# Late rows and first scales written from GpSimd's queue, the norm weight applied to transposed rows

## The chip, the cores and the metric

One core of a Trainium2 chip (TensorE, VectorE, ScalarE, GpSimd and SyncE, with 16 DMA engines). The metric is the device time of one execution, in microseconds (us); less is better. Before the change it is 578.38 us (median of 3 runs, 577.93 to 578.51).

## The reference

Linear attention without a mask, a norm per head, and a mixture of experts with one expert for each token, all in f32:

```python
kv  = einsum('bhsd,bhse->bhde', k, v)          # 8 batches, 8 heads, 576 tokens, 64 wide
out = einsum('bhsd,bhde->bhse', q, kv)
x   = out / sqrt(mean(out*out, -1) + 1e-6) * g_norm     # 4608 tokens x 512
logits = x @ w_gate                            # 8 experts
e_idx  = argmax(logits, axis=1)
gate_w = softmax(logits)[e_idx]
eom    = sigmoid(x @ w_output_gate)
y[token] = gate_w * eom[e_idx] * (relu(x @ w1[e_idx]) @ w2[e_idx])   # 512 -> 1024 -> 512
```

## The kernel before

**Attention.** The 4608 tokens are 36 tiles of 128. For each batch `kv_part` (L598) makes k^T v on TensorE, `out_tile` (L677) multiplies a tile of q with it, and extra columns of the same product give the gate's logits. `evict` in `out_tile` then runs on ScalarE: it copies the tile's row to `xrow` (L686), squares it (L689) and copies the logits (L708). Two tiles share an `xrow`; when the second is copied, `xwrite` (L1076) sends both, 512 KB, to the DRAM tensor `xs`, and gives the slot of `xrow` back at once, so that the next taker has to wait until the write has landed. There are eight such slots, shared with the loads of q, k and v that come late. The rows in `xs` are neither divided by their norm nor multiplied by `g_norm`.

**Routing.** `route` works on four groups of 9, 7, 10 and 10 tiles, on VectorE. It makes the factor of each head, and later the token's scale, in `xtail`, which is written to the DRAM tensor `xt` (16 numbers to a token); for the first two groups `rest_of_scales` does that (L877, two DMAs on ScalarE's queue). It also makes the table of which rows each expert takes.

**Experts.** There are 16 runs: eight over the first 256 rows of each expert, among the first 16 tiles only, then eight over the rest. `run` holds the order written out by hand: `mm1` (L417; for the first pieces `mm1_part`, L392) with `w1`, `mm2` (L453) with `w2`, and between them, at fixed places, the pieces of everything else. The late 20 tiles of attention and the routing of the last two groups are handed out piece by piece in the first seven runs. GpSimd gathers a run's rows (`fetch`, L295, `xg<-xs`) and their tails (`tl<-xr` or `tl<-xt`), each paced by a matmul, multiplies the heads' factors in (L329), and scatters the finished rows (L466). `stage` transposes the rows on TensorE (L362); `stage_hi` takes the transposed tile from PSUM to `xT` on ScalarE (L365), and `stage_lo` makes the rest that the first number leaves, on VectorE (L369). Weights are split in the same way, into `whi` and `wlo`. The first weights are also multiplied by `gcol`, which is `g_norm` laid along the partitions, while they are split: L229 and L256 on ScalarE, L235 and L259 on VectorE. Second weights are split without it (L263, L266, L277, L278).

**What sets the order.** Every engine and queue takes its own list in the order in which the program writes it. SyncE's queue issues all loads, the late row writes among them. A DMA of SyncE or ScalarE waits for one of eight counters, which they use in turn, and thus for an earlier transfer, up to eight back, to land. GpSimd's DMAs have eight counters of their own.

Of the kernel before, what the change touches and what calls it, by code (L numbers as in the profile page):

```python
# [11 lines left out]
F32 = mybir.dt.float32  # L12
F32R = mybir.dt.float32r
BF16 = mybir.dt.bfloat16
I32 = mybir.dt.int32
U32 = mybir.dt.uint32
AF = mybir.ActivationFunctionType
ALU = mybir.AluOpType
# [3 lines left out]
P = 128  # L22
# [3 lines left out]
E = 8  # L26
# [13 lines left out]
EARLY = 16  # L40
# [8 lines left out]
TMAX = 6  # L49
# [5 lines left out]
GMAX = max(GR)  # L55
# [88 lines left out]
def tiles_of(i):  # L144

    _, t0, n = RUNS[i]
    return [(t0 + k, k * P, min(P, n - k * P)) for k in range(-(-n // P))]
# [6 lines left out]
def body(ctx: ExitStack, tc: tile.TileContext, kvm, rem, qT, wg, gn, w1, w2, kc, xs, xr0, xr, xt, tab, out):  # L154
    nc = tc.nc
# [6 lines left out]
    gcol = cst.tile([P, 1], F32, name="gcol")  # L162
# [28 lines left out]
    held = {}  # L191

    def take(shape, dt, name, free=free):

        i = free.pop(0)
        t = mem.tile(shape, dt, name=name, tag=f"slot{i}")
        held[id(t)] = (i, t)
        return t

    def give(t):  # L200
        i = held.pop(id(t))[0]
        (free if i < SLOTS else xfree).append(i)
# [23 lines left out]
    def split_hi(c):  # L226
        r = raw[(0, 1, c)]
        hi = take([P, 1024], F32R, "whi")
        nc.scalar.activation(hi, r, AF.Copy, scale=gcol[:, 0:1])  # L229
        halved[c] = hi  # L230

    def split_lo(c):
        r, hi = raw.pop((0, 1, c)), halved.pop(c)
        lo = take([P, 1024], F32R, "wlo")
        nc.vector.scalar_tensor_tensor(out=lo, in0=r, scalar=gcol[:, 0:1], in1=hi.bitcast(F32),  # L235
                                       op0=ALU.mult, op1=ALU.subtract)
        give(r)
        wgt[(1, c)] = (hi, lo)

    def split(i, which, c, eng=None):  # L240
        r = raw.pop((i, which, c))
        hi = take([P, 1024], F32R, "whi")
        lo = take([P, 1024], F32R, "wlo")
        he, eng = [{"A": nc.scalar, "P": nc.gpsimd, "V": nc.vector}[x] for x in (eng or "AV")]
        if which == 1:
            if eng is nc.gpsimd:

                eng.tensor_scalar(out=r, in0=r, scalar1=gcol[:, 0:1], scalar2=None, op0=ALU.mult)
                if he is nc.scalar:
                    he.copy(hi, r)  # L250
                else:
                    he.tensor_copy(hi, r)
                eng.tensor_tensor(out=lo, in0=r, in1=hi.bitcast(F32), op=ALU.subtract)
            else:
                if he is nc.scalar:
                    he.activation(hi, r, AF.Copy, scale=gcol[:, 0:1])  # L256
                else:
                    he.tensor_scalar(out=hi, in0=r, scalar1=gcol[:, 0:1], scalar2=None, op0=ALU.mult)
                eng.scalar_tensor_tensor(out=lo, in0=r, scalar=gcol[:, 0:1], in1=hi.bitcast(F32),  # L259
                                         op0=ALU.mult, op1=ALU.subtract)  # L260
        else:
            if he is nc.scalar:
                he.copy(hi, r)  # L263
            else:
                he.tensor_copy(hi, r)
            eng.tensor_tensor(out=lo, in0=r, in1=hi.bitcast(F32), op=ALU.subtract)  # L266
        give(r)
        wgt[(which, c)] = (hi, lo)

# [18 lines left out]
    def rows_of(dram, g0, n):  # L288

        r0, w, t = (EARLY, EARLY, g0) if g0 < EARLY else (XE, LATE, g0 - EARLY)  # L290
        return dram[r0:r0 + P * w].rearrange("(m s) x -> m s x", s=w)[:, t:t + n]
# [55 lines left out]
    def stage(i, k):  # L347
        return stage_lo(*stage_hi(i, k))

    def stage_hi(i, k):  # L350
        t, c0, M = tiles_of(i)[k]
        x = xg.pop((i, t))
        if k == 0:
            w = i // E
            n = (ROWS_A, CMAX)[w]
            xT[i] = [rp_[w].tile([P, 4, n], F32R, name="xT", tag=f"xT{j}") for j in range(2)]
        if i or k:
            ps = ps_t.tile([P, 4, P], F32, name="tps", tag="t")
        else:
            ps = pair("tps")[:, 0].rearrange("p (c m) -> p c m", c=4)  # L360
        for c in range(4):
            nc.tensor.transpose(ps[:, c, :M], x[:M, c * P:(c + 1) * P], ident[:M, :M])  # L362
        give(x)
        hi, lo = xT[i]
        nc.scalar.copy(hi[:, :, c0:c0 + M], ps[:, :, :M])  # L365
        return ps, hi, lo, c0, M

    def stage_lo(ps, hi, lo, c0, M):
        return nc.vector.tensor_tensor(out=lo[:, :, c0:c0 + M], in0=ps[:, :, :M],  # L369
                                       in1=hi.bitcast(F32)[:, :, c0:c0 + M], op=ALU.subtract)  # L370

    def half(i):

# [58 lines left out]
    def mm2(i, k, events):  # L432
# [31 lines left out]
        else:  # L464
# [15 lines left out]
    sm = p1.enter_context(tc.tile_pool(name="sm", bufs=2))  # L480
# [5 lines left out]
    xtail = c1.tile([P, NT, TW], F32, name="xtail")  # L486
    nc.gpsimd.memset(xtail, 0.0)
    w = EARLY * DM // P
    nc.gpsimd.dma_start(out=xs[0:EARLY, :].rearrange("o (a x) -> (o a) x", x=w),
                        in_=xtail[:, 0:w // TW, :].rearrange("p n x -> p (n x)"))  # L490
# [29 lines left out]
    for i in range(2):  # L520
        o = c1.tile([P, GMAX + 1, E], BF16, name=f"ohb{i}")
# [113 lines left out]
    def pair(name):  # L635

        nonlocal npair
        pool = (ps_o, ps_p[0])[npair % 2] if ps_p else ps_o
        npair += 1
        return pool.tile([P, 2, 512], F32, name=name, tag="pair")  # L640
# [93 lines left out]
    def route(gi):  # L734
# [5 lines left out]
        n = len(GROUPS[gi])  # L740
        last = gi + 1 == len(GROUPS)
        g0 = GROUPS[gi][0]
        vec = nc.vector

        def pause(k):
            at_pause[0] = k
            yield 1
# [1 line left out]
        lead = gi == EARLY_GROUP  # L749

        a = ss[:, :n]
        y = sm.tile([P, GMAX, E], F32, name="ry")[:, :n]
        vec.tensor_scalar(out=y.bitcast(I32), in0=a.bitcast(I32), scalar1=-0.5,
                          scalar2=float(0x5F3759DF), op0=ALU.mult, op1=ALU.add)
        yield 0
        u = sm.tile([P, GMAX, E], F32, name="ru")[:, :n]
        rv = xtail[:, g0:g0 + n, 0:H]

        q = 0.375 ** 0.5
# [13 lines left out]
        rows_ = rows_of(xt, g0, n)  # L773
# [8 lines left out]
        def scaled(j):  # L782
            w = j.stop - j.start
            eng = nc.gpsimd if gi < EARLY_GROUP and j.start else vec
            eng.tensor_tensor(out=gpv[:, :, j], in0=gpv[:, :, j],
                              in1=rv.unsqueeze(2).to_broadcast([P, n, w, E]), op=ALU.mult)

        def summed(j):
            return vec.tensor_reduce(out=lg[:, :n, j], in_=gpv[:, :, j], axis=AX.X, op=ALU.add)
# [13 lines left out]
        d = sm.tile([P, GMAX, E], F32, name="rd")  # L803
        vec.tensor_tensor(out=d[:, :n], in0=lg[:, :n, 0:E], in1=mx[:, :n].unsqueeze(2).to_broadcast([P, n, E]), op=ALU.subtract)
        yield from pause(3)
        sc = sm.tile([P, GMAX, E], F32, name="rsc")
        scc = cf[:, K_SC:K_SC + E].unsqueeze(1).to_broadcast([P, n, E])
        vec.scalar_tensor_tensor(out=sc[:, :n], in0=d[:, :n], scalar=0.0, in1=scc, op0=ALU.is_equal, op1=ALU.mult)
        yield 0
# [30 lines left out]
        def gate():  # L840
            vec.tensor_tensor(out=og[:, :n], in0=oh[:, :n], in1=lg[:, :n, E:2 * E], op=ALU.mult)
            yield 0
            vec.tensor_reduce(out=ogs[:, :n], in_=og[:, :n], axis=AX.X, op=ALU.add)
            yield 0
            vec.tensor_scalar(out=ogs[:, :n], in0=ogs[:, :n], scalar1=-88.0, scalar2=None, op0=ALU.max)

        def exps():
            nc.scalar.activation(ex[:, :n], d[:, :n], AF.Exp)
            nc.scalar.activation(eo[:, :n], ogs[:, :n], AF.Exp, scale=-1.0)
# [9 lines left out]
        def scales():  # L859
            vec.reciprocal(dn[:, :, :n], dn[:, :, :n])  # L860
            yield 0
            vec.tensor_tensor(out=xtail[:, g0:g0 + n, C_SCALE], in0=se[:, :n], in1=eo[:, :n], op=ALU.mult)

        def rest_of_scales():
            if lead:
                scaled(halves[1])
                summed(halves[1])
            for _ in gate():
                pass
            yield  # L870
            exps()
            for k in range(3):
                norm(k)
            for _ in scales():
                pass
            yield
            nc.scalar.dma_start(out=rows_, in_=xtail[:, g0:g0 + n])  # L877
            yield

        early = g0 < EARLY  # L880
# [21 lines left out]

        if not early:
            exps()
        w = sm.tile([P, GMAX, E], F32, name="rw")
        vec.tensor_tensor(out=w[:, :n], in0=rp[:, :n], in1=oh[:, :n], op=ALU.mult)
        yield 0
        sl = slots[:, g0:g0 + n]
# [32 lines left out]
        yield from low(range(n // 2))  # L941
        if not last:
            yield from pause(7)
        rc = sm.tile([P, GMAX, 3, E * TMAX], BF16, name="rrc")

        def marks(t0, t1, k):
            w = t1 - t0
# [124 lines left out]
    def xwrite(g, o, i):  # L1072
        if not opened[0]:
            xwrites.append((g, o, i))
            return
        nc.sync.dma_start(out=o, in_=i)  # L1076
        if id(i) in held:
            give(i)

# [464 lines left out]
    with ExitStack() as p3:  # L1544
# [4 lines left out]
        with tc.For_i(0, nreg) as i:  # L1549
# [3 lines left out]
            lo = so.tile([P, NT], F32, name="olo")  # L1553
# [26 lines left out]
            ps = pt.tile([P, 4, P], F32, name="ops")  # L1580
# [5 lines left out]
            for f in range(8):  # L1586
                ph = pt.tile([P, P], F32, name="oph")
                for d in range(4):
                    o = d * 256 + (f % 2) * P
# [3 lines left out]
            for f in range(8):  # L1593
                w0 = (f % 2) * DM
                nc.tensor.matmul(py, ht[:, f, :], ws[4 + f // 2][:, w0:w0 + DM], start=(f == 0), stop=(f == 7))
            y = so.tile([P, DM], F32, name="oy")
            nc.scalar.activation(y, py, AF.Copy, scale=tl[:, C_SCALE:C_SCALE + 1])
            nc.gpsimd.indirect_dma_start(out=out, out_offset=bass.IndirectOffsetOnAxis(ap=oi[:, 0:1], axis=0),
                                         in_=y, in_offset=None, bounds_check=NTOK - 1, oob_is_err=False)
# [52 lines left out]
```

## Time and profile before

| | |
|---|---|
| median of 3 runs | 578.38 us |
| the profiled execution | 579.57 us, of which the span of the core 577.6 us |
| TensorE busy (matmul) | 555.5 us, 96% |
| VectorE, ScalarE, GpSimd busy | 358.2, 291.8, 210.6 us |
| granted TensorE clock, mean | 0.991 |
| DMA | 126.32 MB, mean 219 GB/s |

Times inside the trace are counted from the start of the span. TensorE is busy nearly throughout; an engine's idle time matters only where TensorE ends up waiting for it. "Landing" is the time from a DMA's issue to the arrival of its last byte.

### The profile page before, as it was taken

How to read it: one execution, taken by the hardware profiler on the slowest of the kernel's cores; microseconds unless marked ns; L12 is line 12 of the kernel's file. 1: busy time of each engine (PE TensorE's matmuls, PEld its weight loads, DVE VectorE, ACT ScalarE, POOL GpSimd, SP SyncE). 2: the span in 40 equal slices, each digit the busy share in tenths (PEclk: the TensorE clock that was granted, in tenths of full speed). 3: DMA queues.
4: the chain of work that ended last, by engine and by line, in shares of the span. 5: the costliest groups of instructions: out<-in, count | busy, mean ns of one | idle time of the engine just before them, and what ended most of it. 6: DMA issues, size and time to landing. Idle time of an engine off the chain costs nothing.

```text
span 577.6 us, 12048 instructions
## 1 busy us (share of the span) xinstructions
PE 555.5 (96%) x4643; PEld 478.7 (83%) x4643; DVE 358.2 (62%) x695; ACT 291.8 (51%) x546; POOL 210.6 (36%) x204
## 2 busy tenths in 40 slices
PE   6998987999999999999999999999999999999995
PEld 3775786898988898888989889889897988889894
DVE  2268655665588989977696647445365463757540
ACT  1355345676668656745564444434354454635440
POOL 4342333321412341423555525224252443544302
PEclk9999998999999999999999999999999999999998
DMA  8999799887856585676856345256454645556200
GB/s 302 417 417 366 259 414 350 312 302 286 310 204 243 172 312 196 196 240 201 273 197 193 130 146 167 100 169 204 146 173 140 203 151 175 181 174 204 76 5 37
DMA packets 38795, 126.32 MB, mean 219 GB/s; under 512 B 6940, under 2 KB 8333, under 8 KB 38736
## 3 DMA queue, kind: packets, MB, share of 16 engines
q1 hardware_dynamic: 29664, 105.26, 52.2%
q0 software_dynamic: 8352, 19.88, 10.3%
q8 instruction: 38, 0.62, 0.4%
q10 hardware_dynamic: 720, 0.39, 0.2%
q14 instruction: 21, 0.17, 0.1%
HBM read 106.01 MB, written 20.04 MB: 218 GB/s over the span
## 4 chain that ended last, share of the span: by engine, by line
PE 82%; DMA 8%; DVE 3%; issue 3%; ACT 2%; POOL 1%; POOLq 0%; ACTq 0%; SPq 0%
PE hps L417 34%; PE yps L453 32%; PE ops L677 5%; PE tps L362 3%; DMA ld<-kvm 3%; PE kvps L598 3%; PE yps L447 3%; DMA wraw<-w 2%; PE hps L392 2%; DMA gcol<-gn 1%; PE cps L570 1%; DMA xs<-xrow 1%; DVE wlo L278 1%; ACT whi L277 1%; DMA out<-y,oidx 0%
## 5 line engine op out<-in xcount | busy, mean ns | idle before, releaser
L417 PE MATMUL hps<-xT,whi 128*128 128x256 f32 (+8 forms) x992 | 213.7, 308 | 4.7 <-DVE hT L427 4.6
L453 PE MATMUL yps<-whi,hT 128*128 128x512 f32 (+3 forms) x592 | 200.4, 402 | 0.0
L417 PEld LDWEIGHTS hps<-xT,whi 128*128 128x128 f32 x992 | 164.9, 190 | 9.2 <-DVE hT L427 5.8
L417 PE MATMUL hps<-xT,wlo 128*128 128x256 f32 (+8 forms) x496 | 151.1, 305 | 0.0
L453 PEld LDWEIGHTS yps<-whi,hT 128*128 128x128 f32 (+3 forms) x592 | 110.8, 187 | 24.5 <-issue 0.2
L453 PE MATMUL yps<-wlo,hT 128*128 128x512 f32 (+3 forms) x296 | 116.5, 393 | 0.0
L259 DVE SCALAR_TENSOR_TENSOR wlo<-wraw,gcol,whi 128x1024 fp32r<-128x1024 f32 x62 | 83.7, 1352 | 51.5 <-ACT whi L256 51.1
L427 DVE SCALAR_TENSOR_TENSOR hT<-hps,hT 128x256 fp32r<-128x256 f32 (+9 forms) x168 | 63.1, 395 | 84.7 <-ACT hT L425 84.2
L466 POOL DMA_INDIRECT out<-y,oidx x42 | 45.7, 1088 | 179.2 <-ACT y L465 119.0
L425 ACT ACTIVATE hT<-hps 128x256 fp32r<-128x256 f32 (+8 forms) x128 | 54.7, 427 | 105.6 <-PE hps L417 97.5
L417 PEld LDWEIGHTS hps<-xT,wlo 128*128 128x128 f32 x496 | 94.4, 190 | 0.3
L278 DVE TENSOR_TENSOR wlo<-wraw,whi 128x512 fp32r<-128x512 f32 x120 | 90.3, 752 | 3.2
L277 ACT CAST whi<-wraw 128x512 fp32r<-128x512 f32 x120 | 73.4, 612 | 0.0
L256 ACT ACTIVATE whi<-wraw,gcol 128x1024 fp32r<-128x1024 f32 x62 | 71.3, 1151 | 0.1
L329 POOL TENSOR_TENSOR xg<-xg,tl 128x512 f32<-128x512 f32 (+8 forms) x41 | 46.6, 1136 | 57.2 <-DMA tl<-xt,gidx 43.7
L453 PEld LDWEIGHTS yps<-wlo,hT 128*128 128x128 f32 (+3 forms) x296 | 55.5, 187 | 10.4
L295 POOL DMA_INDIRECT xg<-xs,gidx x41 | 43.1, 1052 | 54.3 <-PE hps L417 30.8
L295 POOL DMA_INDIRECT tl<-xt,gidx x41 | 47.4, 1156 | 32.9 <-PE hps L417 18.8
L465 ACT ACTIVATE y<-yps,tl 128x512 f32<-128x512 f32 (+3 forms) x37 | 25.4, 687 | 60.8 <-PE yps L453 48.5
L365 ACT CAST xT<-tps 128x512 fp32r<-128x512 f32 (+8 forms) x42 | 23.0, 548 | 49.9 <-PE tps L362 49.7
L369 DVE TENSOR_TENSOR xT<-tps,xT 128x512 fp32r<-128x512 f32 (+8 forms) x42 | 26.7, 637 | 21.6 <-ACT xT L365 21.4
L677 PE MATMUL ops<-aug,ld 64*64 64x80 f32 (+1 forms) x960 | 33.0, 250 | 3.2 <-ACT gp L708 2.5
(186 smaller groups left out, 456.6 us busy)
## 6 DMA issues: line engine op xcount, KB each, us to landing
wraw<-w SPq DMA_DIRECT2D x128, 512.0 KB, 4.3
ld<-kvm SPq DMA_DIRECT2D x32, 512.0 KB, 8.8
ld<-qT SPq DMA_DIRECT2D x18, 512.0 KB, 8.8
xs<-xrow SPq DMA_DIRECT2D x18, 512.0 KB, 6.1
ld<-rem SPq DMA_DIRECT2D x4, 512.0 KB, 8.5
out<-y,oidx POOLq DMA_INDIRECT x42, 3.1
xg<-xs,gidx POOLq DMA_INDIRECT x41, 4.3
tl<-xt,gidx POOLq DMA_INDIRECT x41, 4.0
```

The costliest lines, as they stand in the source:

```text
L256: he.activation(hi, r, AF.Copy, scale=gcol[:, 0:1])
L259: eng.scalar_tensor_tensor(out=lo, in0=r, scalar=gcol[:, 0:1], in1=hi.bitcast(F32), op0=ALU.mult, op1=ALU.subtract)
L277: nc.scalar.copy(hi[:, h], r[:, h])
L278: nc.vector.tensor_tensor(out=lo[:, h], in0=r[:, h], in1=hi.bitcast(F32)[:, h], op=ALU.subtract)
L295: return nc.gpsimd.indirect_dma_start(out=o[:M, :], out_offset=None, in_=dram[0:XE] if i < E else dram, in_offset=bass.IndirectOffsetOnAxi ...
L329: return eng.tensor_tensor(out=v, in0=v, in1=f, op=ALU.mult)
L417: seq.append(nc.tensor.matmul(ps[:, :C], w[:, o:o + P], x[d][:, :C], start=(d == 0 and k == 0), stop=(d == 3 and k == 2)))
L425: nc.scalar.activation(h[:, 0:C], ps[:, :C], AF.Relu)
L427: nc.vector.scalar_tensor_tensor(out=h[:, l:l + b - a], in0=ps[:, a:b], scalar=0.0, in1=h[:, a:b].bitcast(F32), op0=ALU.max, op1=ALU.subtract)
L453: seq.append(nc.tensor.matmul(ps[:M], a, b, start=(f == 0 and n == 0), stop=(f == 7 and n == 2)))
L466: i_ = nc.gpsimd.indirect_dma_start(out=out, out_offset=bass.IndirectOffsetOnAxis(ap=oidx[i // E][:M, RUNS[i][0], t:t + 1], axis=0), in_=y ...
L677: nc.tensor.matmul(ps[c0:c0 + step_, u, p * W:(p + 1) * W], qt[g // 2][r, p, q0:q0 + step_], augs[b % 3][r, p, :], start=True, stop=True)
```

## The change

Three parts. (1) The late row writes (tiles 16 and up) and the two writes of the first scales go out on GpSimd's queue, in place of SyncE's and ScalarE's. (2) `gcol` is multiplied in when the transposed rows leave PSUM, and the first weights are split like the second ones. (3) Five small tiles of the routing get one buffer in place of two.

```diff
     def split_hi(c):
-        nc.scalar.activation(hi, r, AF.Copy, scale=gcol[:, 0:1])
+        nc.scalar.copy(hi, r)
     def split_lo(c):
-        nc.vector.scalar_tensor_tensor(out=lo, in0=r, scalar=gcol[:, 0:1], in1=hi.bitcast(F32),
-                                       op0=ALU.mult, op1=ALU.subtract)
+        nc.vector.tensor_tensor(out=lo, in0=r, in1=hi.bitcast(F32), op=ALU.subtract)
     def split(i, which, c, eng=None):
-        if which == 1:
...
-                if he is nc.scalar:
-                    he.activation(hi, r, AF.Copy, scale=gcol[:, 0:1])
...
-                eng.scalar_tensor_tensor(out=lo, in0=r, scalar=gcol[:, 0:1], in1=hi.bitcast(F32),
-                                         op0=ALU.mult, op1=ALU.subtract)
+        if he is nc.scalar:
+            he.copy(hi, r)
         else:
...
+            he.tensor_copy(hi, r)
+        eng.tensor_tensor(out=lo, in0=r, in1=hi.bitcast(F32), op=ALU.subtract)
     def stage_hi(i, k):
-        nc.scalar.copy(hi[:, :, c0:c0 + M], ps[:, :, :M])
+        nc.scalar.activation(hi[:, :, c0:c0 + M], ps[:, :, :M], AF.Copy, scale=gcol[:, 0:1])
     def stage_lo(ps, hi, lo, c0, M):
-        return nc.vector.tensor_tensor(out=lo[:, :, c0:c0 + M], in0=ps[:, :, :M],
-                                       in1=hi.bitcast(F32)[:, :, c0:c0 + M], op=ALU.subtract)
+        return nc.vector.scalar_tensor_tensor(out=lo[:, :, c0:c0 + M], in0=ps[:, :, :M], scalar=gcol[:, 0:1],
+                                              in1=hi.bitcast(F32)[:, :, c0:c0 + M], op0=ALU.mult, op1=ALU.subtract)
     def route(gi):
-        y = sm.tile([P, GMAX, E], F32, name="ry")[:, :n]
+        y = sm.tile([P, GMAX, E], F32, name="ry", bufs=1)[:, :n]
...
-            nc.scalar.dma_start(out=rows_, in_=xtail[:, g0:g0 + n])
+            nc.gpsimd.dma_start(out=rows_, in_=xtail[:, g0:g0 + n])
...
     def xwrite(g, o, i):
-        nc.sync.dma_start(out=o, in_=i)
+        (nc.gpsimd if g >= EARLY and id(i) in held else nc.sync).dma_start(out=o, in_=i)
```

The tiles `ru`, `rsc`, `rw` and `rrc` get `bufs=1` as `ry` does.

The change has 18 lines fewer ahead of `stage_hi`, so its line numbers there are lower by 18: L407 is L425 of before, L668 is L686, L277 is L295, L311 is L329, L859 is L877 and L1058 is L1076 (L245 takes the place of L256 and L263). In brackets stands what a row waits for: an engine's progress, or DMAHW0 to 7 (the counters of SyncE's and ScalarE's DMAs) and DMASW0 to 7 (those of GpSimd's).

GpSimd's list behind the first gathers of run 0, before:

```order
L1037 MEMSET issue_mark 128x1
L295 DMA xg<-xs,gidx_74 128x512 [waits DMAHW4_49,PE_49]
L295 DMA tl<-xr,gidx_74 128x16 [waits PE_49]
L295 DMA xg<-xs,gidx_74 128x512 [waits DMASW3_49,Pool_49]
L329 TENSOR_TENSOR xg<-xg,tl 128x512 [waits DMASW2_49,DMASW1_49]
L295 DMA tl<-xr,gidx_74 128x16 [waits PE_49]
L329 TENSOR_TENSOR xg<-xg,tl 128x512 [waits DMASW4_49,DMASW3_49]
L295 DMA tl<-xt,gix_78 128x16 [waits DMAHW4_49,DMAHW3_49,PE_49]
```

and now:

```order
L1019 MEMSET issue_mark 128x1
L1058 DMA xs<-xrow 128x1024 [waits Activation_49]
L277 DMA xg<-xs,gidx_74 128x512 [waits DMAHW4_49,PE_49]
L277 DMA tl<-xr,gidx_74 128x16 [waits DMASW3_49,PE_49]
L277 DMA xg<-xs,gidx_74 128x512 [waits Pool_49]
L859 DMA xt<-xtail 128x112 [waits DVE_49]
L859 DMA xt<-xtail 128x144 [waits DVE_49]
L311 TENSOR_TENSOR xg<-xg,tl 128x512 [waits DMASW3_49,DMASW2_49]
L1058 DMA xs<-xrow 128x1024 [waits DMASW7_49,Activation_49]
L277 DMA tl<-xr,gidx_74 128x16 [waits DMASW0_49,PE_49]
L311 TENSOR_TENSOR xg<-xg,tl 128x512 [waits DMASW4_49,DMASW0_49]
L277 DMA tl<-xt,gix_78 128x16 [waits DMASW5_49,DMASW6_49,DMASW1_49,PE_49]
```

Two row writes and the two writes of the scales now stand among the gathers for run 1; the second row write stands behind a multiplication and ahead of a gather of tails.

ScalarE's list in the first run of the experts, before, where the scales are written:

```order
L708 COPY gp<-ops 128x2x4x16
L425 ACTIVATE hT<-hps 128x256
L877 DMA xt<-xtail 128x112 [waits DMAHW3_49,DVE_49]
L877 DMA xt<-xtail 128x144 [waits DMAHW4_49,DVE_49]
L425 ACTIVATE hT<-hps 128x256 [waits PE_49]
L263 CAST whi<-wraw 128x1024 [waits DMAHW7_49,DMAHW6_49,Activation_49]
```

and a little later, up to the copy of tile 20's row:

```order
L263 CAST whi<-wraw 128x1024 [waits DMAHW0_49]
L609 COPY aug_129<-kvps 128x4x64 [waits DVE_49]
L425 ACTIVATE hT<-hps 128x256 [waits PE_49]
L263 CAST whi<-wraw 128x1024 [waits DMAHW1_49]
L686 COPY xrow<-ops 128x2x4x64 [waits DMAHW5_49,PE_49,Activation_49]
```

and now the whole stretch:

```order
L407 ACTIVATE hT<-hps 128x256
L407 ACTIVATE hT<-hps 128x256 [waits PE_49]
L245 CAST whi<-wraw 128x1024 [waits DMAHW7_49,DMAHW6_49,Activation_49]
L668 COPY xrow<-ops 128x2x4x64 [waits PE_49]
L671 ACTIVATE sq_136<-ops 128x2x4x64
L690 COPY gp<-ops 128x2x4x16
L407 ACTIVATE hT<-hps 128x256 [waits PE_49]
L245 CAST whi<-wraw 128x1024 [waits DMAHW0_49]
L591 COPY aug_129<-kvps 128x4x64 [waits DVE_49]
L407 ACTIVATE hT<-hps 128x256 [waits PE_49]
L245 CAST whi<-wraw 128x1024 [waits DMAHW1_49]
L668 COPY xrow<-ops 128x2x4x64 [waits DMASW7_49,PE_49,Activation_49]
```

The two DMAs are gone from ScalarE's list, and the copy of tile 20's row, which waited for the counter of a row write on SyncE's queue, waits for the counter (DMASW7) of the second row write in GpSimd's list above.

## Rows read from the trace of the kernel before

**Rows 1.** The page's chain that ended last: shares of the span by engine.

```profile
PE 82%; DMA 8%; DVE 3%; issue 3%; ACT 2%; POOL 1%; POOLq 0%; ACTq 0%; SPq 0%
```

**Rows 2.** Stretches: stretch and its us, busy us (and instructions) by engine, granted clock, DMA share, GB/s.

```profile
89.50:92.80 3.30, 3.30 (x42) 2.89 (x41) 2.67 (x5) 1.68 (x5) 1.57 (x1) 0.50 1.00 353
...
99.80:103.10 3.30, 3.30 (x34) 2.65 (x26) 2.70 (x3) 3.30 (x6) 0.64 (x1) 0.50 0.86 351
```

**Rows 3.** Timeline of TensorE: start, us, instruction, idle before and what ended it.

```profile
88.00 0.50 PE L417 MATMUL hps<-xT,whi 128*128 128x256 f32 x2 [2.87 <-DVE hT L427]
99.47 1.15 PE L677 MATMUL ops<-aug,ld 64*64 64x80 f32 x32 [2.51 <-ACT gp L708]
```

**Rows 4.** Timeline of ScalarE and its queue in the same stretch.

```profile
84.86 2.20 ACTq L877 DMA_DIRECT2D xt<-xtail  x2
87.10 0.38 ACT L425 ACTIVATE hT<-hps 128x256 fp32r<-128x256 f32 x1 [5.90 <-DMA xs<-xrow]
88.32 0.59 ACT L686 COPY xrow<-ops 128x512 f32<-128x512 f32 x1
98.05 0.59 ACT L686 COPY xrow<-ops 128x512 f32<-128x512 f32 x1 [4.00 <-DMA xs<-xrow]
```

**Rows 5.** Late row writes on SyncE's queue: the one issued at 74.7, then all 18 row writes.

```profile
L1076 SPq DMA_DIRECT2D xs<-xrow x1: 327/327/327, 74.7 to 74.7; - x1
DMA to landing us min/median/max: 11.9/11.9/11.9
...
DMA to landing us min/median/max: 3.2/6.1/11.9
```

**Rows 6.** Chain in order of time: start, us, what; pieces of TensorE's work at full clock.

```profile
106.83 0.44 PE tps L362 x4
108.32 2.94 PE yps L453 x12
113.78 1.62 PE hps L417 x12
115.41 0.71 PE ops L677 x32
```

**Rows 7.** Timeline of GpSimd, and landings of its gathers at 74.66, 80.17 and 93.14.

```profile
74.66 1.99 POOL L295 DMA_INDIRECT xg<-xs,gidx  x1 [9.37 <-PE hps L392]
84.87 1.04 POOL L329 TENSOR_TENSOR xg<-xg,tl 128x512 f32<-128x512 f32 x1 [3.75 <-DMA tl<-xr,gidx]
93.14 0.99 POOL L295 DMA_INDIRECT tl<-xt,gix  x1
...
DMA to landing us min/median/max: 8.6/8.6/8.6
DMA to landing us min/median/max: 8.2/8.2/8.2
DMA to landing us min/median/max: 5.8/5.8/5.8
```

**Rows 8.** Groups by line and form: busy us, mean ns of one.

```profile
L489 POOL DMA_DIRECT2D xs<-xtail x1 | 0.7, 743 | 0.1
L235 DVE SCALAR_TENSOR_TENSOR wlo<-wraw,gcol,whi 128x1024 fp32r<-128x1024 f32 x2 | 2.6, 1276 | 0.0
L266 DVE TENSOR_TENSOR wlo<-wraw,whi 128x1024 fp32r<-128x1024 f32 x4 | 4.9, 1225 | 1.8 <-ACT whi L263 1.3 <-DMA wraw<-w 0.5
L465 ACT ACTIVATE y<-yps,tl 128x512 f32<-128x512 f32 x34 | 23.4, 687 | 49.3 <-PE yps L453 44.6 <-issue 4.6
L365 ACT CAST xT<-tps 128x512 fp32r<-128x512 f32 x34 | 20.0, 588 | 32.5 <-PE tps L362 32.4
```

**Rows 9.** A later stretch, columns as in rows 2.

```profile
216.00:241.00 25.00, 24.34 (x167) 21.64 (x167) 24.06 (x53) 16.71 (x34) 9.63 (x9) 1.00 0.51 174
```

**Rows 10.** Timeline: ScalarE's first output tile, VectorE's last piece for run 1.

```profile
104.81 0.69 ACT L465 ACTIVATE y<-yps,tl 128x512 f32<-128x512 f32 x1 [0.27 <-PE yps L453]
107.93 0.69 DVE L369 TENSOR_TENSOR xT<-tps,xT 128x512 fp32r<-128x512 f32 x1
```

More of the change, by code (lines that the diff above doesn't have):

```diff
@@ L244, in split @@
         he, eng = [{"A": nc.scalar, "P": nc.gpsimd, "V": nc.vector}[x] for x in (eng or "AV")]
-        if which == 1:
-            if eng is nc.gpsimd:
-                eng.tensor_scalar(out=r, in0=r, scalar1=gcol[:, 0:1], scalar2=None, op0=ALU.mult)
-                if he is nc.scalar:
[L250 to L255, printed above, removed]
-                    he.activation(hi, r, AF.Copy, scale=gcol[:, 0:1])
-                else:
-                    he.tensor_scalar(out=hi, in0=r, scalar1=gcol[:, 0:1], scalar2=None, op0=ALU.mult)
-                eng.scalar_tensor_tensor(out=lo, in0=r, scalar=gcol[:, 0:1], in1=hi.bitcast(F32),
-                                         op0=ALU.mult, op1=ALU.subtract)
-        else:
[L262 to L266, printed above, removed]
+        if he is nc.scalar:
+            he.copy(hi, r)
+        else:
+            he.tensor_copy(hi, r)
+        eng.tensor_tensor(out=lo, in0=r, in1=hi.bitcast(F32), op=ALU.subtract)
         give(r)
@@ L755, in route @@
         yield 0
-        u = sm.tile([P, GMAX, E], F32, name="ru")[:, :n]
+        u = sm.tile([P, GMAX, E], F32, name="ru", bufs=1)[:, :n]
         rv = xtail[:, g0:g0 + n, 0:H]
@@ L805, in route @@
         yield from pause(3)
-        sc = sm.tile([P, GMAX, E], F32, name="rsc")
+        sc = sm.tile([P, GMAX, E], F32, name="rsc", bufs=1)
         scc = cf[:, K_SC:K_SC + E].unsqueeze(1).to_broadcast([P, n, E])
@@ L904, in route @@
             exps()
-        w = sm.tile([P, GMAX, E], F32, name="rw")
+        w = sm.tile([P, GMAX, E], F32, name="rw", bufs=1)
         vec.tensor_tensor(out=w[:, :n], in0=rp[:, :n], in1=oh[:, :n], op=ALU.mult)
@@ L943, in route @@
             yield from pause(7)
-        rc = sm.tile([P, GMAX, 3, E * TMAX], BF16, name="rrc")
+        rc = sm.tile([P, GMAX, 3, E * TMAX], BF16, name="rrc", bufs=1)
         def marks(t0, t1, k):
```

## The prediction

> **What bounds the kernel now.** I read the chain that ended last first. It lies on TensorE for 82% [rows 1], so the time can fall only where TensorE waits or runs slowly. Then its timeline, for idle time before an instruction. Two places stand out, both in run 0 of the experts: it sits idle for 2.87 us until 88.00, waiting for VectorE's eviction of a product, and for 2.51 us until 99.47, waiting for ScalarE to empty the products of an attention tile [rows 3]. The reader is to see that the releasers named there are not the cause. ScalarE's timeline has it: its queue is held at two DMAs that write the first scales, which go out only at 84.86 and just before 87.10, so that an eviction of `hT` starts after 5.90 us of idleness; and the copy of tile 20's row waits 4.00 us, until 98.05, for a row write to land, because its slot is still being read [rows 4]. The write issued at 74.7 on SyncE's queue took 11.9 us to land, where the quickest of the 18 took 3.2 us [rows 5].
>
> The stretch views show a further loss: the granted clock is 0.50, the lower of the two levels (1.2 in place of 2.4 GHz), in 89.50 to 92.80 and again in 99.80 to 103.10, each a little after one of the idle spells [rows 2]. Half speed over 3.3 us loses about 1.65 us each time. The two places thus hold 2.87 + 2.51 + 3.3 = 8.7 us in all. Elsewhere little is open: in 216 to 241 TensorE is busy 24.34 of 25 us, with VectorE busy 24.06 beside it [rows 9].
>
> **The scales' DMAs leave ScalarE.** The order shows the two writes waiting for counters DMAHW3 and DMAHW4, thus for earlier transfers on SyncE's queue. The row write of 74.7 lands at 86.6, which is when the second one goes. On GpSimd they wait for VectorE alone. ScalarE gains up to 5.90 us there, and the eviction that stopped TensorE for 2.87 us starts on time: that stall goes, and with it the reason for the first slow spell. What replaces it on GpSimd is two issues in front of the multiplication at 84.87, which waits for a tail that lands then in any case [rows 7]. A direct DMA of 32 KB over 128 partitions took GpSimd 0.74 us [rows 8]; a gather's issue took up to 1.99 us [rows 7]. Two at 0.74 or even at 1.99 fit between the gather's issue at 80.17 and 84.87; I count nothing. If that cover were gone, the multiplication would be 1 to 2 us later, and its tile is transposed some 9 us on.
>
> **What is late next: tile 20's slot.** This sets the size of the gain. Without stalls TensorE would go from 85.13 (88.00 less 2.87) through 12 matmuls of `mm1` (1.62), an attention tile (0.71), 12 more (1.62), a transposition half as long as the four of 0.44 (0.2), 12 of `mm2` (2.94) and those four (0.44) to tile 21 [rows 3, 6]: 85.13 + 7.5 = 92.7, against 99.47. But tile 21 needs ScalarE to have copied tile 20's row, and that needs the write of tiles 18 and 19 to have landed. That write now stands on GpSimd's list behind the multiplication. The copied row is there at about 83.0 (the copy ended at 88.91, and 5.90 us of waiting goes); GpSimd is free at 84.87 + 1.04 = 85.9 [rows 4, 7], so the write is issued at 85.9.
>
> How long does it take to land? No row write on GpSimd's queue exists in this trace. Bounds: 3.2 us, the quickest on SyncE's queue, and 11.9 us, the slowest [rows 5]. The nearest rows are the gathers of 256 KB from GpSimd in this very stretch, which landed after 8.6 and 8.2 us [rows 7]; 256 KB more at the 353 GB/s that the DMA engines moved here [rows 2] add about 0.7. I take 9.0 us. It lands at 94.9; tile 21 starts 1.42 us later (99.47 less 98.05), at 96.3 instead of 99.47. **Gain 3.1 us.** TensorE now idles from 92.7 to 96.3 in one spell, so I leave the second slow spell in place, moved forward. At the bounds: with 3.2 us the write lands before ScalarE asks (94.05 less 5.90 is 88.2, the write 89.1), tile 21 starts at 92.7, and the gain is 6.8 us, with the clock kept up another 1.65, thus 8.4; with 11.9 us it lands at 97.8 and the gain is 0.3.
>
> The Trainium skill, in "DMA: Bandwidth & Descriptors", section "Issuing engines are not separate DMA queues", speaks against this part: DMAs of all engines run on the same 16 DMA engines, and starting them from another one saves only the time of starting. By that rule the write would land no sooner than on SyncE's queue, and the sum would be the 0.3 us of the upper bound. The trace does not settle it: a gather of 256 KB from GpSimd landed after 8.2 us here, sooner than the write of 512 KB on SyncE's queue with its 11.9, but far later than that queue's best of 3.2 [rows 5, 7].
>
> **The other eight late writes.** They wait for ScalarE's copy in GpSimd's list instead of SyncE's; behind each stand gathers, multiplications or scatters. I price each at 0.74 to 1.99 us of GpSimd, which is busy 9.63 of 25 us in 216 to 241 [rows 9]. TensorE has no stall in these stretches that they would end, and SyncE's loads, freed of them, were not late: nothing.
>
> **The norm weight.** VectorE's split of a first weight falls from 1276 to 1225 ns, 0.05 us; four to a run. Taking `xT` from PSUM on ScalarE rises from 588 to 687 ns, if a scaled copy costs there what it costs for `y` [rows 8]; 0.1 us, two to a run of the first eight. Elsewhere both lie beside TensorE's own work; they are open at two places. The first tile of run 0 stands on the path: 0.1 us lost. In 216 to 241 VectorE is nearly full [rows 9]: 4 x 0.05 = 0.2 us gained. The bounds are a loss of 0.1, if VectorE's gain reaches nobody, and a gain of 0.2, if the first tile has slack; I take a gain of 0.1. The single buffers are used in VectorE's own order, except `rrc`, whose readers on TensorE are done long before the next group; nothing.
>
> **Sum.** 3.1 + 0.1 = 3.2 us. Against the profiled execution, 579.57 us, that gives 576.4; its time stands 1.2 above the median of 578.38, which becomes **575.2 us**.
>
> **Rivals.** *Both stalls go.* If the write lands in 4 to 6 us, ScalarE hardly waits for the slot. For it: writes of that size landed in 3.2 us at best, and the one that took 11.9 stood behind loads in SyncE's queue, which it no longer does. Against: gathers half its size took over 8 us. The gain is 6 to 8.4 us, and at that end, with 0.1 for the weight, the time is 578.4 - 8.5 = 569.9. Chance 0.22.
>
> *The queue changes nothing.* The write lands after 11.9 us, the second wait ends where it did, and the first stall only moves into it: 578.4 - 0.4 = 578.0. That is the page's rule above as a mechanism here. For it: the DMA engines are full, shares near 1.00 [rows 2]. Against: the gather of 256 KB that landed after 8.2 us. Chance 0.15.
>
> *GpSimd's list becomes the bound: slower.* Behind the write of tiles 18 and 19 come a gather of tails, a multiplication, and the tail with the scales of run 0's first output, issued at 93.14 and landing 5.8 us later, at 98.9 [rows 7]. ScalarE needs it at 104.81, and VectorE's last piece for run 1 is done at 108.6 [rows 10], 2.7 us ahead of run 1, which starts when the 12 matmuls from 108.32 end, at 111.3 [rows 6]. If row writes delay that tail by more than 5.9 + 2.7 = 8.6 us, run 1 waits. Two writes at 5.5 us or more of delay each, in one queue, would bring 11 us: 2.4 us lost, and 1.65 in a slow spell behind it, against a gain of 0.4. Time 578.4 + 3.7 = 582.1. For it: the order puts a second write between the tails. Against: a tail behind a write need only wait for its own turn. Chance 0.12.
>
> **How the numbers follow.** My forecast has 0.51. Its own range is the write landing in 6.5 to 11 us: gains of 1.2 to 6, 572.4 to 577.2. A measurement here tells 0.2%, 1.16 us, from no change. Faster by more: nearly all of the forecast and of the first rival, 0.73. Within: the second rival, 0.15. Slower: 0.12. The range leaves out the third rival and the far end of the first, 0.2 in all: 570.5 to 578.6.
>
> **What would show it.** Right: ScalarE's list without a wait at the scales, no idle of 2.87 us near 85, only one stretch at half clock before 110, and one idle spell of 3 to 4 us that ends when the GpSimd write lands, near 95. The landing time of that write is the first thing to read. Wrong: a landing under 6 or over 11 us; a wait of TensorE at run 1's first products for `xT`; GpSimd's issue of a row write well over 2 us.

## The result, and the profile after

The changed kernel took **582.5 us** (median of 11 runs, 579.69 to 586.16), the kernel before 578.62 beside it (11 runs, 577.93 to 586.09). The ratio is 1.0062, with a 95% interval of 1.0043 to 1.0081: 0.6% **slower**, where 575.2 had been forecast. The profiled execution took 582.66 us with a span of 580.5, against 579.57 and 577.6 before; the 2.9 us between the spans are followed below.

The chain that ended last still lies on TensorE, but less of it than in [rows 1], and more on transfers:

```profile
PE 72%; DMA 11%; DVE 6%; issue 5%; ACT 2%; POOL 2%; POOLq 1%; ACTq 0%; DVEq 0%
```

TensorE's timeline, from 60 to 200 us: these are the idle times of over 1 us. The spell before 88.00 of [rows 3] is gone, the one before 99.47 has become 2.08 us before 95.12, and two are new.

```profile
95.12 0.78 PE L659 MATMUL ops<-aug,ld 64*64 64x80 f32 x32 [2.08 <-ACT gp L690]
...
126.61 0.78 PE L659 MATMUL ops<-aug,ld 64*64 64x80 f32 x32 [3.08 <-ACT gp L690]
...
158.66 1.32 PE L659 MATMUL ops<-aug,ld 64*64 64x80 f32 x32 [2.34 <-ACT gp L690]
```

ScalarE's timeline says why. The first row answers to the wait of 5.90 us in [rows 4]: no transfer is waited for any more. The other three are row copies that wait for an earlier row write to land, as one did before.

```profile
82.48 0.38 ACT L407 ACTIVATE hT<-hps 128x256 fp32r<-128x256 f32 x1 [1.08 <-PE hps L399]
...
93.70 0.58 ACT L668 COPY xrow<-ops 128x512 f32<-128x512 f32 x1 [3.85 <-DMA xs<-xrow]
...
125.19 0.58 ACT L668 COPY xrow<-ops 128x512 f32<-128x512 f32 x1 [4.60 <-DMA xs<-xrow]
...
157.24 0.58 ACT L668 COPY xrow<-ops 128x512 f32<-128x512 f32 x1 [4.57 <-DMA xs<-xrow]
```

Stretches of the changed kernel (us, busy time of TensorE, its weight loads, VectorE, ScalarE, GpSimd, then granted clock, DMA share, GB/s). Where [rows 2] have 0.50 the clock is 1.00 now; it is 0.50 behind each of the two new idle spells instead.

```profile
89.50:92.80 3.30, 3.30 (x20) 2.65 (x18) 1.83 (x2) 0.35 (x1) 0.00 (x0) 1.00 1.03 423
99.80:103.10 3.30, 3.30 (x32) 2.53 (x31) 1.74 (x3) 2.38 (x4) 1.90 (x2) 1.00 1.03 416
...
128.10:131.30 3.20, 3.20 (x10) 2.41 (x10) 2.33 (x4) 2.36 (x5) 0.61 (x1) 0.50 0.85 225
...
158.80:162.10 3.30, 3.30 (x42) 3.13 (x42) 2.38 (x5) 2.21 (x7) 0.00 (x0) 0.50 0.08 30
```

The first products of runs 1, 2 and 3 on TensorE's timeline measure what was gained and what was lost. Before:

```profile
111.11 0.40 PE L417 MATMUL hps<-xT,whi 128*128 128x256 f32 x2
...
143.47 0.40 PE L417 MATMUL hps<-xT,whi 128*128 128x256 f32 x2
...
175.93 0.48 PE L417 MATMUL hps<-xT,whi 128*128 128x256 f32 x2
```

After:

```profile
105.26 0.40 PE L399 MATMUL hps<-xT,whi 128*128 128x256 f32 x2
...
142.40 0.40 PE L399 MATMUL hps<-xT,whi 128*128 128x256 f32 x2
...
178.84 0.48 PE L399 MATMUL hps<-xT,whi 128*128 128x256 f32 x2
```

Run 1 starts **5.85 us earlier**. It then lasts 37.14 us instead of 32.36, 4.78 more, and run 2 36.44 instead of 32.46, 3.98 more. That is the two idle spells, 3.08 and 2.34, with about 1.65 of half speed behind each: 4.73 and 3.99. 5.85 - 4.78 - 3.98 = -2.91, the whole difference of the spans. From run 3 to the end the two executions stay about this far apart.

**Why the copies wait.** The write of tiles 22 and 23 tells it; the copy of 125.19, of tile 24's row, waits for it. SyncE's queue before, in that stretch:

```profile
118.39 0.33 SPq L561 DMA_DIRECT2D ld<-qT  x1
118.77 0.43 SPq L220 DMA_DIRECT2D wraw<-w  x1
122.19 0.33 SPq L1076 DMA_DIRECT2D xs<-xrow  x1
122.62 1.80 SPq L561 DMA_DIRECT2D ld<-kvm  x2
124.52 1.21 SPq L220 DMA_DIRECT2D wraw<-w  x2
```

The write waits in the list for ScalarE's copy, and four loads of 512 KB stand behind it. In the changed kernel SyncE no longer waits for the row:

```profile
112.55 0.33 SPq L543 DMA_DIRECT2D ld<-qT  x1
112.92 0.45 SPq L220 DMA_DIRECT2D wraw<-w  x1
113.47 2.59 SPq L543 DMA_DIRECT2D ld<-kvm  x2
116.16 0.86 SPq L220 DMA_DIRECT2D wraw<-w  x2
```

The same four loads leave from 113.47 on, and GpSimd issues the write at 116.62, behind nearly all of them. Before, that one write landed 3.7 us after its issue:

```profile
L1076 SPq DMA_DIRECT2D xs<-xrow x1: 327/327/327, 122.2 to 122.2; - x1
...
DMA to landing us min/median/max: 3.7/3.7/3.7
```

After, 8.5 us:

```profile
L1058 POOL DMA_DIRECT2D xs<-xrow x1: 583/583/583, 116.6 to 116.6; - x1
...
DMA to landing us min/median/max: 8.5/8.5/8.5
```

The packets of the changed kernel by queue from 117.2 (the end of that issue) to 121.1 (packets, MB, share of the 16 engines): q1 carries SyncE's transfers, q0 GpSimd's, and q0 has no line at all. For 3.9 us the write does not begin.

```profile
q1 hardware_dynamic: 320, 1.18, 97.3%
q8 instruction: 1, 0.02, 1.5%
```

From 121.1 to 125.2, up to the landing, the two queues share; q0 carries the write and a gather:

```profile
q1 hardware_dynamic: 224, 0.79, 50.1%
q0 software_dynamic: 242, 0.79, 47.3%
```

The copy of 157.24 waits in the same way, for the write of 148.41, which landed after 8.7 us; the one in its place before, of 149.21, took 4.1 us.

### The profile page after: what moved, and what is told of

Read it like the earlier page. It is cut to its first block, busy times and chain, and to the rows that moved or that the text cites. A ratio compares the mean times of both kernels' runs of the same rounds, so it can differ in the third digit from the quotient of the medians.

```text
span 580.5 us, 12048 instructions
## 1 busy us (share of the span) xinstructions
PE 556.7 (96%) x4643; PEld 479.0 (83%) x4643; DVE 357.6 (62%) x695; ACT 288.9 (50%) x546; POOL 215.2 (37%) x216
## 4 chain that ended last, share of the span: by engine, by line
PE 72%; DMA 11%; DVE 6%; issue 5%; ACT 2%; POOL 2%; POOLq 1%; ACTq 0%; DVEq 0%
PE yps L435 29%; PE hps L399 29%; DMA xs<-xrow 5%; PE ops L659 4%; PE tps L344 3%; PE yps L429 3%; PE kvps L580 2%; PE hps L374 2%; DMA tl<-xt,gidx 2%; DMA ld<-kvm 1%; DMA wgs<-wg 1%; DVE wlo L248 1%; DMA tl<-xr,gidx 1%; DVE wlo L260 1%; PE cps L552 1%
## 5 line engine op out<-in xcount | busy, mean ns | idle before, releaser
L248 DVE TENSOR_TENSOR wlo<-wraw,whi 128x1024 fp32r<-128x1024 f32 x66 | 84.9, 1288 | 46.9 <-ACT whi L245 46.2
L407 ACT ACTIVATE hT<-hps 128x256 fp32r<-128x256 f32 (+8 forms) x128 | 54.8, 428 | 99.3 <-PE hps L399 97.1
L260 DVE TENSOR_TENSOR wlo<-wraw,whi 128x512 fp32r<-128x512 f32 x120 | 91.7, 765 | 3.2 <-ACT whi L259 0.2
L245 ACT CAST whi<-wraw 128x1024 fp32r<-128x1024 f32 x66 | 69.3, 1051 | 0.0
L311 POOL TENSOR_TENSOR xg<-xg,tl 128x512 f32<-128x512 f32 (+8 forms) x41 | 45.1, 1099 | 56.5 <-DMA tl<-xt,gidx 42.2
L277 POOL DMA_INDIRECT xg<-xs,gidx x41 | 43.3, 1056 | 43.0 <-PE hps L399 26.1
L277 POOL DMA_INDIRECT tl<-xt,gidx x41 | 46.4, 1131 | 20.6 <-PE hps L399 16.4
L347 ACT ACTIVATE xT<-tps,gcol 128x512 fp32r<-128x512 f32 (+8 forms) x42 | 27.3, 650 | 53.4 <-PE tps L344 53.4
L351 DVE SCALAR_TENSOR_TENSOR xT<-tps,gcol,xT 128x512 fp32r<-128x512 f32 (+8 forms) x42 | 29.3, 698 | 28.3 <-ACT xT L347 28.0
```

The lines of the kernel that those rows point to most:

```text
L260: nc.vector.tensor_tensor(out=lo[:, h], in0=r[:, h], in1=hi.bitcast(F32)[:, h], op=ALU.subtract)
L277: return nc.gpsimd.indirect_dma_start(out=o[:M, :], out_offset=None, in_=dram[0:XE] if i < E else dram, in_offset=bass.IndirectOffsetOnAxi ...
L311: return eng.tensor_tensor(out=v, in0=v, in1=f, op=ALU.mult)
L407: nc.scalar.activation(h[:, 0:C], ps[:, :C], AF.Relu)
```

## The experiments

Two theories had to be told apart from each other and from rivals. **S** (slots): the loss is the copies' wait for a slot whose write has not landed. **O** (order): that write is late because SyncE's loads, which used to stand behind it, now go out ahead of it. Rivals were **W**, the move of the norm weight; **L**, a GpSimd list that ends late; and **G**, that GpSimd's queue itself is slow for such a write.

**1. Which part loses.** Four kernels beside 29 runs of the kernel before (median 579.05).

All late rows back to SyncE:

```diff
-        (nc.gpsimd if g >= EARLY and id(i) in held else nc.sync).dma_start(out=o, in_=i)
+        nc.sync.dma_start(out=o, in_=i)
```

> All writes of late rows go back to SyncE's queue; the scales' DMAs stay on GpSimd's queue and the norm weight stays in the transposed rows. Theory S (a row write on GpSimd's queue lands late, and the copy that wants its slot waits): the two TensorE stalls of the changed kernel at 126.6 (3.08 us) and 158.7 (2.34) go with their two half-clock spells (1.7 us each), 8.8 us in all; the stall at 99.5 of the kernel before (2.5 us and 1.7 of its spell) may come back, since the write of tiles 18 and 19 is behind the loads again: span 572 to 576, ratio to before 0.990 to 0.996. Rival W (the weight's move costs the time): still in, so 580 or more, ratio 1.003 or more. Rival L (GpSimd's list, its gathers and tails, ends late): the list loses eight issues of 0.57 us, most of it stays, ratio above 1.000.

579.95 us, ratio 1.0013 (0.9995 to 1.0031). The two late spells are gone, as S says, but the early one has grown. The profiled execution took 586.73 us: from 20 to 35 us its granted clock was 0.50, so that its times from there on stand some 7 us later than in the others. ScalarE and TensorE:

```profile
104.46 0.58 ACT L668 COPY xrow<-ops 128x512 f32<-128x512 f32 x1 [8.13 <-DMA xs<-xrow]
```

```profile
105.88 1.34 PE L659 MATMUL ops<-aug,ld 64*64 64x80 f32 x32 [6.22 <-ACT gp L690]
```

The window from 104.2 to 110.8 of this run, granted clock third from the end:

```profile
104.20:110.80 6.60, 4.92 (x41) 3.98 (x42) 4.13 (x5) 6.34 (x12) 2.46 (x3) 0.50 0.90 367
```

With the scales off ScalarE its copies come sooner, but SyncE writes tiles 18 and 19 no sooner. The first stall only moves into the second: no gain without the early part of the row writes. The forecast of 572 to 576 for the span was too low because it let the early stall come back at 2.5 us; it came back at 6.22.

Only the first two row writes on GpSimd's queue:

```diff
-        (nc.gpsimd if g >= EARLY and id(i) in held else nc.sync).dma_start(out=o, in_=i)
+        (nc.gpsimd if g in (EARLY, EARLY + 2) and id(i) in held else nc.sync).dma_start(out=o, in_=i)
```

> Only the writes of tiles 16/17 and 18/19 stay on GpSimd's queue, the other late rows are written by SyncE's; all else as in the changed kernel. Theory S: keeps the 5.85 us that the changed kernel has gained at the start of run 1 and has no stalls at 126.6 and 158.7: 5.85 less nothing, span 571.5 to 573.5, ratio 0.989 to 0.993, and no worse than with all rows back. Rival W: 580 or more. Rival L: between 576 and 580.

**573.18 us, ratio 0.9899** (0.9866 to 0.9932): the eight later writes alone make the difference between a gain of 1% and a loss of 0.6%. W had 580 or more for this kernel and L 576 to 580; neither is met. Of all row copies one still waits, at 93.39, before the gain is made:

```profile
ACT xrow L668 <- DMA xs<-xrow: 3.7, 1, 3.7
```

The norm weight alone (the changed kernel with both queues as before):

```diff
-        (nc.gpsimd if g >= EARLY and id(i) in held else nc.sync).dma_start(out=o, in_=i)
+        nc.sync.dma_start(out=o, in_=i)
...
-            nc.gpsimd.dma_start(out=rows_, in_=xtail[:, g0:g0 + n])
+            nc.scalar.dma_start(out=rows_, in_=xtail[:, g0:g0 + n])
```

> The kernel before with the norm weight's move alone (and the smaller buffers); both queues as before. Theory S: the weight's move is worth nothing, ratio 0.999 to 1.001, stalls at 88.0 and 99.5 as before. Rival W: the loss is here, ratio 1.005 or more.

578.67 us, ratio 0.998 (0.9955 to 1.0004), with both old stalls in place (2.73 us before 88.06, 2.39 before 99.39): W falls.

A ninth slot, all writes on GpSimd:

```diff
-XSLOTS = 8
+XSLOTS = 9
```

> The changed kernel with nine slots for the row chunks and late loads in place of eight; every write stays on GpSimd's queue. Theory S: writes still land 5 to 9 us after their issue, but a copy takes a slot that came free one step earlier, so its wait of 4.6 us at 125 and at 158 goes, with both stalls: span 571.5 to 574, ratio 0.989 to 0.994. If instead the writes hurt by the DMA engines' time that they take from loads, or GpSimd's list is late, or the weight's move costs: as the changed kernel, ratio 1.004 to 1.008.

578.47 us, 0.9986 (0.9963 to 1.0008), half way. The copy of 157.24 no longer waits; that of 124.08 still does, 4.21 us, perhaps because the late loads take slots from the same list and may take the ninth. This left S neither shown nor refuted.

**2. Slots and order.** Four kernels beside 22 runs of the kernel before (median 578.71).

The row writes alone, made from the kernel before:

```diff
-        nc.sync.dma_start(out=o, in_=i)
+        (nc.gpsimd if g >= EARLY and id(i) in held else nc.sync).dma_start(out=o, in_=i)
```

> The kernel before with the late row writes alone moved to GpSimd's queue; the scales' DMAs stay on ScalarE's and the weight in the first weights. Theory S: the stall at 88.0 (2.87 us and 1.7 of its spell) stays, the one at 99.5 loses about 2 us, and the two new ones at 126 and 158 come (3.1 and 2.3 us with 1.7 us of spell each): about 5 to 7 us more than before, ratio 1.006 to 1.014. Rival: the new stalls come from the scales' DMAs on GpSimd's queue or from the start of run 1 5.85 us earlier; then they are not here and the ratio is 0.993 to 1.000.

585.32 us, 1.0118 (1.0078 to 1.0157). The early stall stays and both late ones are there, with the scales' DMAs on ScalarE's queue and run 1 starting at 108.67, only 2.44 us earlier than before. Behind the two late stalls the granted clock stayed at 1.00, so the slow stretches that the forecast counted behind each are missing from this profile. TensorE:

```profile
88.73 0.80 PE L417 MATMUL hps<-xT,whi 128*128 128x256 f32 x2 [3.68 <-DVE hT L427]
...
130.10 0.78 PE L677 MATMUL ops<-aug,ld 64*64 64x80 f32 x32 [3.16 <-ACT gp L708]
...
160.38 0.78 PE L677 MATMUL ops<-aug,ld 64*64 64x80 f32 x32 [2.20 <-ACT gp L708]
```

The eight later writes on ScalarE's queue:

```diff
-        (nc.gpsimd if g >= EARLY and id(i) in held else nc.sync).dma_start(out=o, in_=i)
+        (nc.gpsimd if g in (EARLY, EARLY + 2) and id(i) in held else nc.scalar
+         if g >= EARLY and id(i) in held else nc.sync).dma_start(out=o, in_=i)
```

> The changed kernel with the eight later row writes issued by ScalarE, on its queue, instead of GpSimd; the first two stay on GpSimd's. Theory O (the write lands late because SyncE no longer waits for the row and sends its loads ahead of it): SyncE's list is as free as in the changed kernel, so the writes at 116 and 148 still land after 7 to 9 us and the copies wait 3 to 5 us; ratio 1.000 to 1.008. Rival G (GpSimd's own queue is slow, for its descriptors or its start): they land after 3.5 to 4.5 us, no stall, ratio 0.988 to 0.992.

581.22 us, 1.0038 (1.0011 to 1.0066): G falls. The write issued at 149.07 landed after 8.4 us, where the same one took 8.7 on GpSimd's queue, and copies wait 4.59 and 3.97 us as on GpSimd's queue. Packets by queue from 116.5, where the issue of the earlier write ends, to 121 (q10 is ScalarE's):

```profile
q1 hardware_dynamic: 368, 1.33, 93.0%
q10 hardware_dynamic: 13, 0.05, 2.9%
```

SyncE's next load held until the row's copy is done (the mark is set in `xwrite`, taken by the next load):

```diff
+        if g > EARLY + 2 and id(i) in held:
+            hold[0] = copied[0]
```

> The changed kernel, every late row write on GpSimd's queue, but SyncE's next load after each of the eight later writes waits for the row's last copy, as it did when the write stood in SyncE's list. Theory O: no load is sent ahead of the write, which lands after 5 to 6.5 us in place of 8.5; copies wait under 2 us, no stall over 1.5 us at 126 and 158, ratio 0.988 to 0.994. Rival G: it lands after 8 us or more as in the changed kernel, ratio 1.003 to 1.008.

580.05 us, 1.0025 (0.9997 to 1.0053). That is near G's forecast, and the copies still wait 3.85 and 5.02 us. SyncE's queue shows that the edit did not do what it was meant to (L551 is L543 of the changed kernel, L1066 below is L1058):

```profile
116.28 0.80 SPq L551 DMA_DIRECT2D ld<-kvm  x2
117.18 2.49 SPq L220 DMA_DIRECT2D wraw<-w  x2
```

GpSimd issued the write from 116.55 to 117.14, and two loads had gone from 116.28 on. A lead of a quarter of a microsecond was enough: from 117.2 to 121 none of GpSimd's packets moved here either, against 218 of SyncE's. The test is mended below.

A ninth slot that loads may not take:

```diff
-XSLOTS = 8
+XSLOTS = 9
...
-                load(late_loads, xfree, 1)
+                load(late_loads, xfree, 2)
...
-        load(late_loads, xfree, 1)
+        load(late_loads, xfree, 2)
```

> The changed kernel with nine slots, and late loads that leave two of them free instead of one, so that the ninth goes to the rows (with nine slots alone a load could take it). Theory S: the writes still land after 7 to 9 us, but no copy waits over 1 us for one, no stall at 126 and 158: ratio 0.988 to 0.994. If the loss were the traffic itself or GpSimd's late lists: as with nine slots alone, 0.997 to 1.001.

573.24 us, **0.9911** (0.9881 to 0.994). The write issued at 143.09 still took 8.4 us to land, and no row copy waits for one. S is shown: in this kernel a late landing costs only through the slot. L falls with it, for GpSimd's list is as long here as in the changed kernel.

**3. The order itself, and the remedies together.** Four kernels beside 17 runs of the kernel before (median 579.01).

The load waits for a memset that stands behind the write on GpSimd:

```diff
+        if g > EARLY + 2 and id(i) in held:
+            hold[0] = nc.gpsimd.memset(issue_mark, 0.0)
```

> As the run with held loads, but the load waits for a one-element memset that stands behind the write's issue in GpSimd's list, so that no load can leave SyncE before the write has been issued (with the row's copy as the mark two loads left at 116.28 and 116.7, and the write at 116.55). Theory O (loads issued ahead of the write delay it, whatever the queue): its first packets move within 2 us of the issue, it lands after 4.5 to 6.5 us, no stall over 1.5 us at 126 and 158: span 571 to 574, ratio 0.987 to 0.994. Rival G (the queue itself): lands after 7.5 us or more, ratio 1.001 to 1.006.

573.99 us (median of 4), **0.9899** (0.9868 to 0.993), with eight slots and every late row on GpSimd's queue. SyncE's loads:

```profile
117.32 1.12 SPq L551 DMA_DIRECT2D ld<-kvm  x2
```

That is 1.04 us later than with the copy as the mark (116.28), and behind the issue of 116.59. The write's landing:

```profile
L1066 POOL DMA_DIRECT2D xs<-xrow x1: 586/586/586, 116.6 to 116.6; - x1
...
DMA to landing us min/median/max: 6.0/6.0/6.0
```

Packets by queue from 117.2 to 119.0, where the changed kernel has none in q0:

```profile
q0 software_dynamic: 97, 0.39, 65.5%
q1 hardware_dynamic: 33, 0.10, 14.1%
```

The copy waits 2.1 us, and TensorE no longer for it. O is shown: same queue, same write, loads behind it instead of ahead, and 2.5 us of landing and some 8 us of the time are back (582.5 to 574.0).

First two writes on GpSimd, the rest on SyncE, and the spare slot (the edits of "Only the first two row writes" and of "A ninth slot that loads may not take" together):

> The first two late writes on GpSimd's queue, the other eight on SyncE's, and a spare slot for the rows. Theory S: each of the two remedies alone removes the two late stalls and gave 573.2; together they save only the 1.2 us before tile 20: 571 to 573.5, ratio 0.987 to 0.992. Rival: the spare slot delays a load and a wait for it comes: 574 to 577.

573.02 us, 0.9887 (0.9863 to 0.9911), the lowest median of the study, but not to be told from either remedy alone.

All rows on SyncE, with the spare slot:

> All rows written by SyncE, scales' DMAs on GpSimd, norm weight moved, and the spare slot. Theory S: tile 20 does not wait for the write of tiles 18 and 19 any more, so the stall of 6.2 us and its 3.4 us of half clock go: 580 less 8 to 9, 570.5 to 574, ratio 0.986 to 0.992; then no row write need leave SyncE. Rival: SyncE, held by the row, sends loads late (a wait for kvm or w of over 2 us): 575 to 579.

575.87 us, 0.993 (0.9904 to 0.9956), 2 us over the forecast range. The copies wait no more, but neither the theory nor its rival named what is late next. ScalarE's first output of run 0 waits for its tail, and behind it the piece that run 1 needs:

```profile
102.03 0.69 ACT L447 ACTIVATE y<-yps,tl 128x512 f32<-128x512 f32 x1 [4.51 <-DMA tl<-xt,gix]
...
103.71 0.68 ACT L347 ACTIVATE xT<-tps,gcol 128x512 fp32r<-128x512 f32 x1
```

TensorE starts run 1 after that:

```profile
104.44 0.38 PE L399 MATMUL hps<-xT,whi 128*128 128x256 f32 x1 [1.70 <-ACT xT L347]
```

The same wait stands in the run with the spare slot and every row on GpSimd's queue (4.86 us). But there GpSimd issues that tail's gather at 95.65 instead of 96.75, TensorE idles 0.68 us instead of 1.70, and the clock stays at 1.00; here it is 0.52 from 105.7 to 109.0. About 1.0 us of idleness and 1.6 of half speed make up the 2.6 us between the two medians.

Both queues as before, with the spare slot:

> Both queues as before, norm weight moved, and the spare slot. Theory S: the stall of 2.9 us at 88.0 (the scales' DMAs on ScalarE's queue wait for the write of tiles 16 and 17) stays with its half clock, the one at 99.5 (2.5 us and 1.7) goes: 573.5 to 575.5, ratio 0.991 to 0.995, slower than with the scales on GpSimd's queue by 1 to 4.5 us. Rival: the spare slot alone is the whole gain, equal to that run within 0.5 us.

575.64 us, 0.9926 (0.99 to 0.9952). The time is at the upper end of what S said, but the order of the two kernels is not as S said: with the spare slot, moving the scales alone gained nothing that can be told, and the rival's "within 0.5 us" holds (0.23). The trace shows what each of them pays: here a stall of 3.21 us before 88.36, there the one just shown.

## Why the prediction was wrong

**The step that failed** is "The other eight late writes": "TensorE has no stall in these stretches that they would end, and SyncE's loads, freed of them, were not late: nothing." They cost 4.78 + 3.98 = 8.76 us: with the loads ahead of them, two of these writes landed after 8.5 and 8.7 us instead of 3.7 and 4.1, and the copies that needed their slots waited 4.60 and 4.57 us. The step asked which stall the move would end, and what a load gains by going sooner. It did not ask what the loads would now go ahead of. It had the means: the rule applied to the write of tiles 18 and 19, that a copy waits for the landing of an earlier write, can hold for every pair of tiles, and the section on the kernel before says that the eight slots are shared. The landing of 9 us that the prediction itself took for GpSimd's queue had only to be tried on the next writes. Before, tile 24's row was copied 0.4 us after the write of 122.19 had landed:

```profile
126.32 0.60 ACT L686 COPY xrow<-ops 128x512 f32<-128x512 f32 x1
```

With 9.0 us instead of 3.7 that copy would have waited 4.9 us, an estimate from these rows; 4.60 were measured.

**The scales.** Right. GpSimd issues both in 1.14 us at 82.39, and the wait of 5.90 us and the stall of 2.87 us are gone. The multiplication behind them stands at 85.77 instead of 84.87, for which the prediction counted nothing; no stall came of it in this kernel. But this gain is not its own: without the early row writes (1.0013) it went into the next wait.

**Tile 20's slot.** The mechanism was right and the size off. The write was issued at 86.76 (85.9 forecast), and landed after 6.8 us, where 9.0 had been taken; the copy that waits for it started at 93.70; tile 21 came at 95.12 instead of 96.3, and without the slow spell that was left in. 3.1 + 1.2 + 1.65 = 5.95, against the 5.85 measured at run 1. GpSimd's timeline has these:

```profile
82.39 1.14 POOL L859 DMA_DIRECT2D xt<-xtail  x2
85.77 1.04 POOL L311 TENSOR_TENSOR xg<-xg,tl 128x512 f32<-128x512 f32 x1 [2.24 <-DMA tl<-xr,gidx]
86.76 0.57 POOL L1058 DMA_DIRECT2D xs<-xrow  x1
```

**The price of a write on GpSimd** was bounded by 0.74 and 1.99 us; it is 0.56 to 0.62 for the ten, below both. It was never the question.

**The norm weight**: 0.1 us forecast, and alone 0.998 with an interval that holds 1; too small to tell.

**The rivals.** The early part alone came out inside the forecast's own range, near its better end: a landing of 6.8 us (6.5 to 11) and 5.85 us gained (1.2 to 6). "Both stalls go" wanted a landing in 4 to 6 us and 6 us or more; with one remedy the kernel takes 573 us, just short of it. "GpSimd's list becomes the bound" gave 582.1, close to the 582.5 measured, but by coincidence: its place, the tail of run 0's first output, is not where this kernel lost. That place is real, though, as the run with all rows on SyncE and the spare slot shows. For "the queue changes nothing" the prediction named the Trainium skill, "DMA: Bandwidth & Descriptors", section "Issuing engines are not separate DMA queues": DMAs of all engines run on the same 16 DMA engines. It was weighed on the one write that did gain. For the eight later ones the runs agree with it: on ScalarE's queue a write landed after 8.4 us, on GpSimd's the same one after 8.7, as long as the same loads had been issued ahead.

## What to carry to other kernels

A transfer that waits in a queue's list also holds back what stands behind it; before it is moved to another queue, list what then goes out ahead of it, and ask who waits for its landing. Where a buffer is given back at the issue of its write, a later taker that finds no other free pays what is left of the landing time, so try a changed landing time on each of them, not only on the one that stalls now. Here the loss could be cured at either end, by the order of issues (0.9899) or by one more buffer that nothing else may take (0.9911).

## What the runs showed of the hardware

For its first microseconds a write on a queue of its own got no share of the DMA engines, or hardly any, while they worked on loads issued before it: none of GpSimd's packets moved in 3.9 us, and 13 of ScalarE's against 368 of SyncE's in 4.5 us. Then it shared: GpSimd's queue moved 242 packets against 224 in the next 4.1 us, although SyncE's loads issued at 116.16, half a microsecond ahead of the write, landed only after 10.4 us. So not every load issued ahead went ahead, and what decides it is not shown. With the loads issued after it, the write began at once: 97 of GpSimd's packets moved in 1.8 us against 33.

Half clock followed some of TensorE's idle spells and not others. Behind the spells before 126.61 and 158.66 the granted clock was 0.50; behind the one of 2.08 us before 95.12 it stayed at 1.00, and behind 3.16 and 2.20 us in the run with the row writes alone too. It also came behind short spells alone: in the run with all rows back it was 0.50 from 20 to 35 us, with TensorE busy throughout and idle for 1.03 and 0.47 us at most in the four microseconds before. What decides it is not shown. From 20 to 560 us of the run with the spare slot it was 1.00:

```profile
20.00:560.00 540.00, 533.96 (x4448) 464.33 (x4447) 354.01 (x682) 285.72 (x539) 208.55 (x196) 1.00 0.63 221
```
